# Reordering the start of a fused attention and GLU kernel: wo loaded early, fewer warm-ups, two clamps moved, a split wait

## The chip, the cores and the metric

The kernel runs on one core of one Trainium2 chip. The metric is the device time of one execution in microseconds (us): the median of the runs, less is better. Five engines work side by side, each through its own list of instructions in order: PE (TensorE, matmuls; its weight loads are shown as PEld), DVE (VectorE), ACT (ScalarE), POOL (GpSimd) and SP (SyncE, which here only issues DMA transfers). They wait for each other through semaphores.

## The reference

One sequence of 2048 tokens of width 448, all in bf16: a block of linear attention, then a GLU block, each behind a layer norm and with a residual.

```python
def _A_ref(x, wqkv, wo):                       # 16 heads of 28
    q, k, v = ...                              # x @ wqkv
    phi = lambda t: jnp.where(t > 0, t + 1, jnp.exp(t)) + 1e-6
    pq, pk = phi(q), phi(k)
    kv = jnp.einsum("bhsd,bhse->bhde", pk, v)
    z = jnp.einsum("bhsd->bhd", pk)
    num = jnp.einsum("bhqd,bhde->bhqe", pq, kv)
    den = jnp.einsum("bhqd,bhd->bhq", pq, z)[..., None] + 1e-6
    return (num / den).transpose(...) @ wo
def _B_ref(x, w_gate, w_up, w_down):
    return (_gelu(x @ w_gate) * (x @ w_up)) @ w_down
h = x + _A_ref(_layernorm(x), A_wqkv, A_wo)
h2 = h + _B_ref(_layernorm(h), w_gate, w_up, w_down)
```

## The kernel before, in words

The tokens are cut into 16 tiles of 128. Every piece of work is a task with a name, and the table ORDERS at the top lists, for each engine in turn (PE, ACT, DVE, POOL, SP), the names in the order in which that engine issues them. Nothing else decides the order. What a task waits for follows from the buffers that it reads and writes: `_Graph.add` collects these, and `emit` puts a wait ahead of the task for each semaphore that it has not yet seen far enough. A task with `mw` places its waits inside itself: each buffer has the number of the matmul that needs it.

The names, in order of time (t is a tile):

- **Warm-up.** warm1 (16 small matmuls) and warm0 (WARM matmuls of 128 columns, L454) use ones only and feed nothing.
- **Loads.** dx0 to dx12 bring x on the sync queue, dwk and dwv the key and value weights on ACT's queue; dwq with dwq_t and dwq_u the query weights, pqones a row of ones for the divisor; dwo, dwo_t, dwo_u and dwo_s the four pieces of wo (336, 56, 56 and 336 KB), dwg and dwu the gate and up weights, dwd the down weights.
- **First norm.** bnst and bnag (DVE) give mean and variance, ln and rstd (ACT) the inverse deviation, negm (POOL) the negated mean, norm the normed tile xn (DVE for tiles 0 to 3, POOL for the rest), dup (ACT) a copy of its last columns. Tiles 0 to 3 are transposed on PE (tr, L495) and copied out by ACT (ev, L523); from tile 4 on a DMA transposes them (xT, L526).
- **Keys and values.** k and v (8 and 6 matmuls of 64 rows, in pairs on the two halves of the PE rows, L430) fill two PSUM banks per tile. ek (ACT) takes the exponential of the keys, cl (L566) clamps it, ph (DVE, L568) makes phi(k) in the tile pk; evv (ACT, L570) copies the values. acc (halves a and b) adds phi(k) times v into banks 6 and 7. The a and b halves write the same banks from the other row half, so a task that follows one of the other kind on the same banks waits until PE has finished that one. Below this is called a turn of the row halves. The same holds between k and v of a tile, qa and qb, woa and wob, nda and ndb.
- **Queries.** qa and qb give four groups of heads for 512 tokens. For the first three of eight such pairs eq (ACT), cq (POOL) and pq (DVE, L627) make phi(q); for the others eq and rq (ACT, L616, L617), then cq and pq (DVE, L618, L619). kz1 and kz2 (DVE) take the finished sums out of banks 6 and 7.
- **Attention output and second norm.** nd multiplies phi(q) with the sums, rd and om (DVE) divide; for tiles 0 and 1 PE transposes the result (tro), ACT copies it (evo), wo multiplies; hr (DVE, L660) adds the residual, hbnst and hbnag and hln and hrstd give the norm, normh the normed tile hn, and wrap (L695) copies its first 64 columns behind its last. trh (7 transposes, L702) and evh (ACT or DVE) bring tiles 0 and 1 into hnT. The other tiles go in pairs, with DMA transposes oT and hT, and with POOL for vpe, pow, hnegm and normh.
- **GLU.** gu computes gate and up of one chunk of columns into a pair of banks, of which there are two; ge (ACT, L830) takes the Gelu of the gate, hm (DVE, L832) the product; the next but one gu needs the pair back. tbl2 loads the Gelu table once, behind the exponentials up to eq14. down multiplies with the down weights, out (DVE) adds the residual, dout stores.

Of the kernel before, what the change touches and what calls it, by code (L numbers as in the profile page):

```python
# [7 lines left out]
ALU = mybir.AluOpType  # L8
# [53 lines left out]
)  # L62


class _Buf:
    __slots__ = ("name", "writer", "readers")

    def __init__(self, name):
        self.name = name
        self.writer = None  # L70
        self.readers = []


# [157 lines left out]
def bass_sequential_preLN__linear_attn_block__glu_gated_geglu__prompt_kernel(  # L231
    nc, A_x, A_wqkv, A_wo, B_x, B_w_gate, B_w_up, B_w_down, out, cfg=None
):
    cfg = dict(cfg or {})
# [7 lines left out]
    HN_R = 4  # L242
    HR = 8
    O_R = 4
    QCH = 512
    NQC = S // QCH
    N_PE_TR = 4
    STAT_GROUPS = [[0], [1], [2], [3]] + [[t, t + 1] for t in range(4, T, 2)]
    EV_DVE = cfg.get("ev_dve", ())
    N_DVE_NORM = cfg.get("n_dve_norm", 4)  # L250
    N_PE_A2 = 2
    B1_CHUNKS = [2, 2, 4, 4, 4]
    WARM = 38
    WARM2 = 8
# [658 lines left out]
```

## Time and profile before

| what | value |
|---|---|
| median of 3 runs | 196.42 us |
| the runs | 196.16, 196.42, 196.70 us |
| the profiled execution | 196.70 us, of which the span 194.9 us |
| PE busy | 190.3 us (98%) |
| DVE, ACT, POOL busy | 116.3, 78.2, 42.0 us |
| granted TensorE clock over the span | 0.999 |
| DMA traffic | 17.53 MB, mean 90 GB/s |

All times of the trace count from the start of the span. A row of the timeline gives the start, the length, the engine, the line in the source, the operation, the tile that it writes and those that it reads, and in brackets how long its engine stood idle before it and who ended that. The ends of matmuls are modelled, so a PE that is shown busy can hold short waits; they show as idle time of PEld. Instructions of one line in a row are merged into one row, with their number (x6).

### The profile page before, as it was taken

The numbers are of one execution on the slowest core, as the hardware profiler recorded it, in microseconds if no ns is written. First come the engines' busy times: TensorE is split into PE (matmuls) and PEld (weight loads), VectorE is DVE, ScalarE is ACT, GpSimd is POOL, SyncE is SP. The second block draws the span as 40 slices with busy tenths as digits, with TensorE's granted clock in tenths as the row PEclk, the third lists the DMA queues.
The fourth block names the chain that finished last, engine by engine and source line by source line (L and its number), as shares of the span: only waits on it lengthen the run. The fifth ranks groups of instructions, "written<-read, shape, count | busy, mean of one in ns | idle before, by whom it ended". The sixth has DMA issues, their size and how long they took to land.

```text
span 194.9 us, 5336 instructions
## 1 busy us (share of the span) xinstructions
PE 190.3 (98%) x2192; PEld 137.9 (71%) x2192; DVE 116.3 (60%) x301; ACT 78.2 (40%) x205; POOL 42.0 (22%) x90
## 2 busy tenths in 40 slices
PE   7999999999999999999999999999999999999994
PEld 7556658754588977976675577877778779899554
DVE  2989735368998946843967745756735443431512
ACT  3689866669784212220442441233232442411100
POOL 3099974300050310500500500500500000000000
PEclk9999999999999999999999999999999999999999
DMA  6944558999836052152062250172040000010111
GB/s 191 377 116 97 81 110 185 247 248 205 260 103 110 15 101 50 50 105 62 10 129 46 46 106 2 30 117 51 5 94 28 23 0 0 3 47 3 47 47 47
DMA packets 37256, 17.53 MB, mean 90 GB/s; under 512 B 28272, under 2 KB 36336, under 8 KB 37232
## 3 DMA queue, kind: packets, MB, share of 16 engines
q1 hardware_dynamic: 36352, 16.45, 36.8%
q10 hardware_dynamic: 880, 0.75, 1.2%
q8 instruction: 17, 0.28, 0.6%
q14 instruction: 7, 0.06, 0.1%
HBM read 8.72 MB, written 1.84 MB: 54 GB/s over the span
## 4 chain that ended last, share of the span: by engine, by line
PE 96%; issue 1%; ACT 1%; DVE 1%; POOL 0%; DVEq 0%; ACTq 0%; POOLq 0%
PE ps L430 87%; PE ps L780 6%; PE ps L454 2%; DVE x_sb L660 1%; PE ps L495 1%; ACT xn L617 1%; PE ps L681 0%; ACT xnT L523 0%; PE ps L672 0%; DVE x_sb L756 0%; POOL ones_bf L395 0%; POOL eps_t L398 0%; ACT pqT L616 0%; DVEq L196 0%; ACTq L196 0%
## 5 line engine op out<-in xcount | busy, mean ns | idle before, releaser
L430 PE MATMUL ps<-hnT,wgu_sb 64*128 64x512 bf16 (+1 forms) x980 | 90.4, 333 | 0.0
L430 PEld LDWEIGHTS ps<-hnT,wgu_sb 64*128 64x128 bf16 x980 | 64.5, 94 | 18.6 <-DVE hh L832 1.7
L830 ACT ACTIVATE gl<-ps 128x256 bf16<-128x256 f32 x112 | 36.9, 381 | 89.3 <-PE ps L430 88.2
L832 DVE TENSOR_TENSOR hh<-ps,gl 128x256 bf16<-128x256 f32 x112 | 42.5, 415 | 35.7 <-ACT gl L830 31.5
L430 PE MATMUL ps<-wd_sb,hh 64*128 64x448 bf16 x336 | 34.4, 349 | 0.0
L430 PEld LDWEIGHTS ps<-wd_sb,hh 64*128 64x128 bf16 x336 | 25.6, 94 | 6.2 <-DVE x_sb L756 0.2
L430 PE MATMUL ps<-wkv_sb,xnT 64*128 64x448 bf16 x192 | 22.4, 350 | 0.4 <-ACT xnT L523 0.4
L462 DVE BATCH_NORM_STATS2 st<-x_sb 128x6 f32<-128x448 bf16 x32 | 18.7, 611 | 2.6 <-DMA x_sb<-in_A_x_dram 2.6
L756 DVE TENSOR_TENSOR x_sb<-ps,x_sb 128x448 bf16<-128x448 f32 (+1 forms) x17 | 9.9, 591 | 16.6 <-PE ps L430 9.8
L474 POOL TENSOR_SCALAR ln<-mv 128x2 f32<-128x2 f32 x7 | 1.6, 223 | 75.0 <-DVE mv L463 74.9
L568 DVE SCALAR_TENSOR_TENSOR pk<-ps,tm 128x448 bf16<-128x448 f32 x16 | 9.8, 620 | 9.6 <-POOL tm L566 7.1
L430 PE MATMUL ps<-xnT,wq_sb 64*128 64x512 bf16 x112 | 14.9, 377 | 0.2 <-ACT xn L617 0.2
L430 PEld LDWEIGHTS ps<-wkv_sb,xnT 64*128 64x128 bf16 x192 | 10.1, 94 | 6.3 <-issue 0.8
L430 PE MATMUL ps<-wo_sb,oT 64*128 64x448 bf16 x98 | 12.1, 350 | 0.1
L660 DVE TENSOR_TENSOR x_sb<-ps,x_sb 128x448 bf16<-128x448 f32 x16 | 9.4, 618 | 4.6 <-PE ps L430 4.4
L780 PE MATMUL ps<-wd_sb,hh 128*128 128x448 bf16 (+1 forms) x70 | 10.8, 315 | 0.0
L566 POOL TENSOR_SCALAR tm<-e 128x448 bf16<-128x448 bf16 x16 | 8.9, 559 | 6.4 <-ACT e L565 5.5
L487 POOL TENSOR_SCALAR hn<-x_sb,nm,rs 128x448 bf16<-128x448 bf16 x14 | 10.0, 720 | 0.8 <-POOL rs L476 0.2
L565 ACT ACTIVATE e<-ps 128x448 bf16<-128x448 f32 x16 | 8.5, 541 | 3.5 <-PE ps L430 2.2
L780 PEld LDWEIGHTS ps<-wd_sb,hh 128*128 128x128 bf16 x70 | 6.7, 98 | 4.3 <-issue 0.4
L655 DVE TENSOR_TENSOR o_sb<-ps,rd 128x448 bf16<-128x448 f32 x16 | 9.4, 612 | 0.1
L570 ACT ACTIVATE v<-ps 128x448 bf16<-128x448 f32 x16 | 8.4, 542 | 2.1 <-PE ps L430 2.1
(69 smaller groups left out, 140.4 us busy)
## 6 DMA issues: line engine op xcount, KB each, us to landing
out_dram<-x_sb SPq DMA_DIRECT2D x15, 112.0 KB, 1.7
wgu_sb<-in_B_w_gate_dram SPq DMA_DIRECT2D x7, 224.0 KB, 6.1
wgu_sb<-in_B_w_up_dram SPq DMA_DIRECT2D x7, 224.0 KB, 6.4
wd_sb<-in_B_w_down_dram SPq DMA_DIRECT2D x1, 1568.0 KB, 8.3
x_sb<-in_A_x_dram SPq DMA_DIRECT2D x2, 448.0 KB, 5.3
wkv_sb<-in_A_wqkv_dram ACTq DMA_DIRECT2D x2, 336.0 KB, 3.7
x_sb<-in_A_x_dram SPq DMA_DIRECT2D x3, 224.0 KB, 4.2
wo_sb<-in_A_wo_dram SPq DMA_DIRECT2D x2, 336.0 KB, 4.4
```

The lines of the kernel that those rows point to most:

```text
L430: ins = e.matmul(o_, l_, r_, start=s_, stop=p_, **kw)
L462: op("dve", lambda e: e.bn_stats(st[:, t, :], src_ap), [b_src], [b_st[t]], "%sbnst%d" % ("" if mv is mv1 else "h", t), 0.53, key, after=after)
L487: return lambda e: e.tensor_scalar(dst, src[:, t, :], nm[:, t:t + 1], rs[:, t:t + 1], ALU.add, ALU.mult)
L565: act_exp(lambda e: e.activation(e1[:, ie, :], oK, AF.Exp), bank(bk), [b_e1[ie]], "ek%d" % t, _c_act(D), kk)
L566: op("pool", lambda e: e.tensor_scalar(tm1[:, ie, :], e1[:, ie, :], 1.0 + EPS, 0.0, ALU.min, ALU.max), [b_e1[ie]], [b_tm1[ie]], "cl%d" % t ...
L568: op("dve", lambda e: e.scalar_tensor_tensor(pk[:, i, :, 0:GW], psK3, EPS, tm1[:, ie, :].rearrange("p (g e) -> p g e", g=NG), ALU.max, ALU ...
L655: op("dve", lambda e: e.tensor_tensor(o_sb[:, so, oc:oc + D].rearrange("p (a e) -> p a e", e=28), nd3[:, :, 0:28], rd[:, i, :].unsqueeze(2 ...
L660: op("dve", lambda e: e.tensor_tensor(h_sb[:, u, :], ps[:, b, 0:D], x_sb[:, u, :], ALU.add), bank(b) + [b_x[u]], [b_h[u]], "hr%d" % u, 0.5 ...
L756: op("dve", lambda e: e.tensor_tensor(x_sb[:, t, c0:c1], ps[:, bk, c0:c1], h_sb[:, t, c0:c1], ALU.add), bank(bk) + [b_h[t]], [bo], "out%d% ...
L780: ins = e.matmul(ps[:, bk, c0:c1], hh[:, j, hsl(t)], wd_sb[:, j, c0:c1], start=(j == 0), stop=(j == NJ - 1))
L830: G.add("act", lambda e, gi=gi, cs_=cs_, psG=psG: e.activation(gl[:, gi, cs_], psG[:, cs_], AF.Gelu_apprx_tanh), r=bank(BK_G[i]), w=[b_glh ...
L832: op("dve", lambda e, dst=dst, srcU=srcU, srcL=srcL: e.tensor_tensor(dst, srcU, srcL, ALU.mult), bank(BK_U[i]) + [b_glh], [b_ar[j_][t % HR ...
```

## The change

Four edits of the source and a new table:

- dwo, dwo_t, dwo_u and dwo_s move from behind the last xT to the list of first loads, behind dwq_u; pqones and xT4 now follow them, and dwg0 follows xT15 directly. The data and its destination stay as they are.
- WARM goes from 38 to 33.
- cl14 and cl15 run on DVE; the operation is the same.
- trh waits in two places: for normh ahead of the first transpose, for wrap ahead of the seventh, the only one that reads the copied columns.
- ORDERS is new on every engine. On DVE, pkones moves ahead of the first bnst; on PE, acc3a, acc4a, acc8b, acc9b, acc10a, acc13a, acc14a and qb31 change places, among others; on ACT, ek15 comes before evv15 and eq14 behind evh0. The diff ends with one line of PE's list; the places that the prediction speaks of are shown there.

```diff
-    WARM = 38
+    WARM = 33
+    CL_DVE = cfg.get("cl_dve", (14, 15))
...
         dma(wq_sb[64:128, 3, 0:D], A_wqkv[384:448, 0:D], [b_wq[2]], "dwq_u", 64 * D * 2, first=True)
+        dma(wo_sb[:, 0:3, :], A_wo[0:384, :].rearrange("(g p) n -> p g n", p=128), [b_wo[0]], "dwo", 384 * D * 2, first=True)
+        dma(wo_sb[0:64, 3, :], A_wo[384:448, :], [b_wo[1]], "dwo_t", 64 * D * 2, first=True)
+        dma(wo_sb[64:128, 3, :], A_wo[0:64, :], [b_wo[2]], "dwo_u", 64 * D * 2, first=True)
+        dma(wo_sb[:, 4:7, :], A_wo[64:448, :].rearrange("(g p) n -> p g n", p=128), [b_wo[3]], "dwo_s", 384 * D * 2, first=True)
...
         prev = xts[-1:]
-        prev = [dma(wo_sb[:, 0:3, :], A_wo[0:384, :].rearrange("(g p) n -> p g n", p=128), [b_wo[0]], "dwo", 384 * D * 2, after=prev, key=19.0)]
...
-            op("pool", lambda e: e.tensor_scalar(tm1[:, ie, :], e1[:, ie, :], 1.0 + EPS, 0.0, ALU.min, ALU.max),
-               [b_e1[ie]], [b_tm1[ie]], "cl%d" % t, 0.53, kk)
+            op("dve" if t in CL_DVE else "pool", lambda e: e.tensor_scalar(tm1[:, ie, :], e1[:, ie, :], 1.0 + EPS, 0.0, ALU.min, ALU.max),
+               [b_e1[ie]], [b_tm1[ie]], "cl%d" % t, _c_dve(D, 4.0) if t in CL_DVE else 0.53, kk)
...
-            def ftrh(e):
+            def ftrh(e, W):
                 ins = None
-                for k in (0, 1, 2, 4, 5, 6, 3):
+                for n, k in enumerate((0, 1, 2, 4, 5, 6, 3)):
+                    if n in (0, 6):
+                        W(n)
...
-            G.add("pe", ftrh, r=[b_hn[sh], b_hnd[sh], b_ident], w=bank(bh), name="trh%d" % t, dur=_c_mm(128, 7), key=ka)
+            G.add("pe", ftrh, r=[b_hn[sh], (b_hnd[sh], 6), b_ident], w=bank(bh), name="trh%d" % t, dur=_c_mm(128, 7), key=ka, mw=True, pdt=_c_mm(128))
...
-    " v5 k6 qa01 v6 qb01 k7 acc3a acc4a v7 acc4b acc5b k8 acc5a acc6a v8 k9 k10 v9 v10 qa10 acc6b acc7b qb10 acc7a"
+    " v5 acc3a k6 qa01 v6 qb01 acc4a k7 acc4b acc5b v7 k8 acc5a acc6a v8 k9 k10 v9 v10 qa10 acc6b acc7b qb10 acc7a"
```

More of the change, by code (lines that the diff above doesn't have):

```diff
@@ L15 @@
     "warm1 warm0 tr0 tr1 k0 v0 k1 tr2 tr3 v1 k2 acc0a k3 v2 v3 qa00 acc0b acc1b qb00 k4 acc1a acc2a v4 k5 acc2b acc3b"
[4 rows of a table removed]
[4 rows of a table added]
     " wo6b down0b nd8a gu11 nd8b gu10 gu13 gu12 down2a wo8a down2b wo8b gu15 nd10a gu14 nd10b gu17 gu16 gu19 gu18 gu21"
     " wo10a wo10b gu20 nd12a gu23 nd12b gu22 gu25 gu24 gu27 gu26 wo12a down4a wo12b gu29 nd14a gu28 nd14b gu31 down4b"
[40 rows of a table removed]
[31 rows of a table added]
+    "ones eps mhalf mones powwarm ident mask_a opad mask_b mask_c negm4 cl0 norm4 norm5 negm6 cl1 norm6 norm7 negm8"
[8 rows of a table added]
 )
@@ L531, in bass_sequential_preLN__linear_attn_block__glu_gated_geglu__prompt_kernel @@
         prev = xts[-1:]
-        prev = [dma(wo_sb[:, 0:3, :], A_wo[0:384, :].rearrange("(g p) n -> p g n", p=128), [b_wo[0]], "dwo", 384 * D * 2, after=prev, key=19.0)]
-        prev = [dma(wo_sb[0:64, 3, :], A_wo[384:448, :], [b_wo[1]], "dwo_t", 64 * D * 2, after=prev, key=19.0)]
-        prev = [dma(wo_sb[64:128, 3, :], A_wo[0:64, :], [b_wo[2]], "dwo_u", 64 * D * 2, after=prev, key=19.0)]
-        prev = [dma(wo_sb[:, 4:7, :], A_wo[64:448, :].rearrange("(g p) n -> p g n", p=128), [b_wo[3]], "dwo_s", 384 * D * 2, after=prev, key=19.0)]
         for k in range(7):
```

83 rows, old and new, of the table ORDERS are left out of this document.

## The prediction

> **What bounds the kernel now.** First the page: the span, and the engines' shares of the chain that ended last. Then the view by stretches (start:end, length, then busy time and instructions of PE, PEld, DVE, ACT and POOL, granted clock, DMA share, GB/s).
>
> ```profile
> span 194.9 us, 5336 instructions
> PE 96%; issue 1%; ACT 1%; DVE 1%; POOL 0%; DVEq 0%; ACTq 0%; POOLq 0%
> 0.00:12.00 12.00, 10.53 (x136) 7.68 (x138) 7.89 (x25) 6.99 (x20) 3.82 (x17) 1.00 0.80 261
> 12.00:30.00 18.00, 18.00 (x230) 10.93 (x226) 13.05 (x30) 14.83 (x46) 16.40 (x32) 1.00 0.54 90
> 30.00:55.00 25.00, 24.42 (x300) 14.99 (x297) 17.10 (x41) 18.28 (x29) 3.98 (x7) 1.00 0.94 237
> 55.00:180.00 125.00, 124.88 (x1455) 96.50 (x1451) 73.69 (x199) 37.44 (x112) 17.84 (x35) 1.00 0.24 49
> ```
>
> PE carries 96% of the chain. From 55 to 180 us it misses 0.12 us, so the many reordered names of the second half have nothing to win there. What can move lies before 55: 1.47 us without PE work up to 12 us, and 0.58 us between 30 and 55. Inside "busy" PE time lie some more short waits, which show as idle time of the weight loads (PEld). I take the change's places in order of time.
>
> **1. Five fewer warm-ups.** Rows of the timeline (start, length, engine, line): the warm-ups, norm0, the memset of pk, rstd1, norm1, tr0 with tr1, k0, tr2 with tr3, and for later use a DVE copy with the PE operation that waited for it.
>
> ```profile
> 1.93 4.24 PE L454 MATMUL ps<-ones_bf 128*128 128x128 bf16 x38
> 5.21 0.37 DVE L486 TENSOR_SCALAR xn<-x_sb,mv,rs 128x448 bf16<-128x448 bf16 x1
> 5.58 0.27 DVE L399 MEMSET pk<- 128x256 bf16 x1
> 5.66 0.20 ACT L469 ACTIVATE rs<-ln 128x1 f32<-128x1 f32 x1
> 5.97 0.40 DVE L486 TENSOR_SCALAR xn<-x_sb,mv,rs 128x448 bf16<-128x448 bf16 x1
> 6.10 0.96 PE L495 MATMUL ps<-ident,xn 64*128 64x64 bf16 x20
> 7.43 0.74 PE L430 MATMUL ps<-wkv_sb,xnT 64*128 64x448 bf16 x6 [0.36 <-ACT xnT L523]
> 9.76 0.75 PE L495 MATMUL ps<-ident,xn 64*128 64x64 bf16 x20
> 51.95 0.18 DVE L695 COPY hn<-hn 128x64 bf16<-128x64 bf16 x1
> 52.15 0.78 PEld L702 LDWEIGHTS ps<-ident,hn 128*128 128x128 bf16 x14 [0.37 <-DVE hn L695]
> ```
>
> norm0 is done at 5.21 + 0.37 = 5.58, but tr0 starts at 6.10, behind the warm-ups. Five of them take 5 x 4.24/38 = 0.56 us, so their end would allow 5.54. PE answers a finished DVE operation in 0.02 us (51.95 + 0.18 to 52.15). So tr0 starts at 5.60, 0.50 earlier, and now waits for norm0. Behind it on PE stand tr1 and k0, and k0 also waits for ev0, ScalarE's copy of tr0's result (the 0.36 us of idle time in its row): all of it moves with tr0, and k0 goes from 7.43 to 6.94, **+0.49**. tr1 gains less, as norm1 needs rstd1, done at 5.86: the memset moved out from ahead of norm1 (0.27 us, now in DVE's idle time before the first x tile) frees nothing. But tr1 at 6.39 still serves k1 in time, which stands behind k0 and v0.
>
> This holds for the profiled execution, where the tensor engine ran slowly until after tr1: 0.112 us per 128-column warm-up, and tr0 with tr1 took 0.96 us where tr2 with tr3, the same work, took 0.75. The clock column reads 1.00 there, so the rows decide. In an execution that reaches the fast rate during the warm-ups, these end earlier by themselves and the five are worth less, down to nothing. The three runs spread from 196.16 to 196.70, and the profiled one is the slowest. [...]
>
> **2. wo ahead of the first transpose.** The sync queue, before and after, from wq on (DMA rows; the transposes are xT4 to xT15):
>
> ```order
> L364 DMA wq_sb<-in_A_wqkv_dram 64x448 x2
> L364 DMA pqT<-ones_bf 1x64x128
> L526 DMA_TRANSPOSE xnT<-xn 128x4x128 x12
> L364 DMA wo_sb<-in_A_wo_dram 128x3x448
> L364 DMA wo_sb<-in_A_wo_dram 64x448 x2
> L364 DMA wo_sb<-in_A_wo_dram 128x3x448
> L364 DMA wgu_sb<-in_B_w_gate_dram 64x1792
> ```
> ```order
> L365 DMA wq_sb<-in_A_wqkv_dram 64x448 x2
> L365 DMA wo_sb<-in_A_wo_dram 128x3x448
> L365 DMA wo_sb<-in_A_wo_dram 64x448 x2
> L365 DMA wo_sb<-in_A_wo_dram 128x3x448
> L365 DMA pqT<-ones_bf 1x64x128
> L531 DMA_TRANSPOSE xnT<-xn 128x4x128 x12
> L365 DMA wgu_sb<-in_B_w_gate_dram 64x1792
> ```
>
> Four loads now stand ahead of xT4, and the gate and up weights directly behind xT15.
>
> ```profile
> 9.50:10.50 1.00, 1.00 (x28) 0.66 (x24) 0.53 (x2) 1.00 (x5) 0.56 (x1) 1.00 1.09 374
> 11.00:13.00 2.00, 2.00 (x26) 1.10 (x26) 2.00 (x8) 1.92 (x7) 2.00 (x5) 1.00 0.01 3
> 6.88 0.60 SPq L364 DMA_DIRECT2D pqT<-ones_bf  x1
> 11.65 10.30 SPq L526 DMA_TRANSPOSE xnT<-xn  x7
> 15.52 0.79 PE L430 MATMUL ps<-wkv_sb,xnT 64*128 64x448 bf16 x6
> L364 SPq DMA_DIRECT2D wo_sb<-in_A_wo_dram x4: 487/594/1370, 28.6 to 31.2; - x4
> DMA to landing us min/median/max: 2.4/2.5/4.1
> ```
>
> Issuing costs 4 x 0.6 = 2.4 us of the sync queue, from 6.88 to about 9.3, before xT4 can be issued (11.65, or 11.2 in step with k0). The data is 784 KB, 0.80 MB, at 374 GB/s 2.1 us. The engines are full until nearly 11 and empty from 11 to 13 (3 GB/s), so wo ends at about 12.9. xT4 lands 2.5 us after issue, at 13.7 to 14.2; the wanted k4 is at 15.52 - 0.49 = 15.03. Bounds: nothing, if the issue and the bulk overlap; 0.4 us, if all 2.5 us came behind 12.9. I take **0**, nearer to the former, as most of the 2.5 us is issue (1.2 us or more each: 10.30 for 7). Later, wgu comes 3.2 us sooner, but nobody waits for it: PE lists no wait for a DMA at all.
>
> **3. The chain of clamps into k6.** Everything that feeds k6 must move up too, and GpSimd has little room (16.40 of 18 us busy from 12 to 30). The clamps cq1 and cq0, DVE's pq1 and pq0, two negm, and k6's weights:
>
> ```profile
> 16.75 1.19 POOL L626 TENSOR_SCALAR tm<-e 112x512 bf16<-112x512 bf16 x2
> 17.39 1.29 DVE L627 SCALAR_TENSOR_TENSOR pqT<-ps,tm 112x512 bf16<-112x512 f32 x2
> 17.91 0.40 POOL L481 TENSOR_SCALAR nm<-mv 128x2 f32<-128x2 f32 x2
> 18.74 0.12 PEld L430 LDWEIGHTS ps<-wkv_sb,xnT 64*128 64x128 bf16 x4 [0.29 <-DVE pqT L627]
> ```
>
> k6 takes its banks from pq1 and pq0 (17.39 + 1.29 = 18.68) and starts at 18.74. GpSimd works through without a break from cl1 on, and the new order puts the same operations ahead of cq0 as the old one, and negm12 besides (0.40 / 2 = 0.20). If its chain starts 0.49 sooner, as cl0 and norm4 hang on k0 and v0, cq0 ends at 16.75 + 1.19 - 0.49 + 0.20 = 17.65 and pq0, half of 1.29 and a hand-over of 0.1 behind it, at 18.4. PE would reach k6 at 18.74 - 0.49 = 18.25, or at 18.37 with acc3a's four matmuls, which now stand ahead of it (half of the 0.23 us that eight such loads take in step 4). With the answer time k6 starts at about 18.5: **-0.13** (bounds 0, and -0.4 if GpSimd's chain gains nothing by k0).
>
> **4. The last two clamps, 36 to 41 us.** DVE at the end of the K tiles (L566, L568, L642 and L643 of before are clamp, pk, kz1 and kz2):
>
> ```order
> L568 SCALAR_TENSOR_TENSOR pk<-ps,tm 128x4x112 x5
> L642 TENSOR_TENSOR kvz<-ps,mask 113x16x28
> L643 TENSOR_TENSOR kvz<-ps,mask 113x16
> ```
> ```order
> L569 SCALAR_TENSOR_TENSOR pk<-ps,tm 128x4x112 x3
> L567 TENSOR_SCALAR tm<-e 128x448
> L569 SCALAR_TENSOR_TENSOR pk<-ps,tm 128x4x112
> L567 TENSOR_SCALAR tm<-e 128x448
> L569 SCALAR_TENSOR_TENSOR pk<-ps,tm 128x4x112
> L644 TENSOR_TENSOR kvz<-ps,mask 113x16
> L643 TENSOR_TENSOR kvz<-ps,mask 113x16x28
> ```
>
> The two clamps come onto DVE, each ahead of its pk, and on ScalarE ek15 changes places with evv15. Rows: evv14 with evv15, ek15, cl15, ph15, qa20's weights, the weights of acc12b, and the copy group of DVE (busy, mean ns).
>
> ```profile
> 37.08 0.98 ACT L570 ACTIVATE v<-ps 128x448 bf16<-128x448 f32 x2
> 37.93 0.56 ACT L565 ACTIVATE e<-ps 128x448 bf16<-128x448 f32 x1
> 38.58 0.56 POOL L566 TENSOR_SCALAR tm<-e 128x448 bf16<-128x448 bf16 x1 [0.75 <-ACT e L565]
> 39.27 0.62 DVE L568 SCALAR_TENSOR_TENSOR pk<-ps,tm 128x448 bf16<-128x448 f32 x1 [0.68 <-PE ps L430]
> 38.11 0.12 PEld L430 LDWEIGHTS ps<-xnT,wq_sb 64*128 64x128 bf16 x4 [0.25 <-ACT v L570]
> 37.59 0.23 PEld L430 LDWEIGHTS ps<-v,pk 64*128 64x128 bf16 x8 [0.22 <-PE ps L430]
> L749 DVE COPY hn<-hn 128x448 bf16<-128x448 bf16 x14 | 3.5, 273 | 1.0 <-POOL hn L487 0.9
> ```
>
> No row shows the clamp on DVE; the copy of the same size takes 0.27 us and norm0, above, 0.37. With 0.27 (its operands are constants, so it is nearer to the copy), the clamp saves 0.29 us and the hand-over of 0.13 between 39.14 and 39.27, and ek15's new place half of the 0.85 between 37.08 and 37.93: ph15 ends at 39.0 and not at 39.89. But PE did not wait so long for it. qa20 waits for evv15 (38.11), which now comes behind ek15 and so about 0.44 us **later**. Behind qa20 stand two acc halves less (13a and 14a are now ahead of it, 0.12 each as above), and no turn between acc15b and acc15a (0.22, paid earlier, beside that wait, between acc13b and acc13a): 0.24 + 0.22 - 0.44 gives **+0.02** (bounds -0.2 if the earlier turn is not hidden, and +0.3 if evv15 comes in time).
>
> **5. The late wait, 49 to 57 us.** PE from the last wo of tiles 2 and 3 to the first gate and up matmuls:
>
> ```order
> L430 MATMUL ps<-wo_sb,oT 128x448 x8
> L430 MATMUL ps<-xnT,wq_sb 128x512 x6
> L430 MATMUL ps<-wo_sb,oT 128x448 x6
> L702 MATMUL ps<-ident,hn 128x128 x14
> L430 MATMUL ps<-kvz,pqT 128x116 x16
> ```
> ```order
> L435 MATMUL ps<-wo_sb,oT 128x448 x14
> L705 MATMUL ps<-ident,hn 128x128 x14
> L435 MATMUL ps<-xnT,wq_sb 128x512 x6
> L435 MATMUL ps<-kvz,pqT 128x116 x16
> ```
>
> qb31 (six matmuls) moves behind the hn transposes and fills the wait ahead of nd4a. Rows: the weights of nd4a and of wo4b, eq14, the table load, the first Gelu, and the group of q matmuls.
>
> ```profile
> 53.47 0.21 PEld L430 LDWEIGHTS ps<-kvz,pqT 49*128 49x128 bf16 x7 [0.34 <-DVE x_sb L660]
> 62.84 0.12 PEld L430 LDWEIGHTS ps<-wo_sb,oT 64*128 64x128 bf16 x4 [0.50 <-PE ps L430]
> 51.69 1.02 ACT L616 ACTIVATE pqT<-ps 112x1024 bf16<-112x1024 f32 x1 [0.35 <-PE ps L430]
> 54.08 1.28 ACT L850 ACT_TABLE_LOAD   x1
> 55.87 0.66 ACT L830 ACTIVATE gl<-ps 128x256 bf16<-128x256 f32 x2 [0.50 <-PE ps L430]
> L430 PE MATMUL ps<-xnT,wq_sb 64*128 64x512 bf16 x112 | 14.9, 377 | 0.2 <-ACT xn L617 0.2
> ```
>
> The wait of 0.34 us goes. But wo2a and wo2b now adjoin and pay a turn as wo4a and wo4b do (0.50), so the hn transposes move up by 6 x 14.9/112 - 0.50 = 0.3 us, and gu1 by some 0.1. The seventh transpose alone now waits for its wrap copy, which DVE does behind normh0; it comes while the other six run, and trh0 and qb31 queue behind it for less than 0.2. What decides is ScalarE. evh0 ended at the table load's start, 54.08, and now ends at 53.78; eq14 (1.02) has moved in between, so the table load runs from 54.8 to 56.1 and not to 55.36, and the first Gelu starts 0.2 us later than 55.87 did. gu3 needs the bank that this Gelu and its product free; so the 0.1 is lost: **0** (bounds -0.25 and +0.35).
>
> **Sum.** 0.49 + 0 - 0.13 + 0.02 + 0 = 0.38 us on the profiled execution, 196.70 (its span 194.9 and 1.8 around it): 196.32. On a run like the lowest, 196.16, the first term is gone: 196.16 + 0.13 - 0.02 = 196.27. Both lie near 196.3, so I forecast **196.3**, against a median of 196.42. A measurement of this kernel can tell about 0.3%, 0.59 us, from no change: this is inside.
>
> **The rivals.**
> - More is won (195.6, chance 0.25): k6 finds its banks free, and of the waits in 4 and 5 the 0.22 and 0.34 us go without new ones: 196.70 - 0.49 - 0.22 - 0.34. For: DVE has idle time in 36 to 41. Against: the turns and the table load above.
> - The gain is eaten by xT4 or k6 (196.7, 0.12): 0.4 us more at either place, on 196.3.
> - The clock rises one step late (197.8, 0.13): with the warm-ups ending 0.5 us sooner, the slow rate lasts past k0. k0, v0 and k1 fill the time from 7.43 to 9.76, 2.33 us; at half rate that much more at most, less what their own waits hide, and nothing if the rate rises at k0: I take 1.5, on 196.3. [...] For: the rate was still slow in tr0, at 6.10, four us after the first warm0 matmul. Against: the gap ahead of k0 shrinks as well. [...]
>
> **How the numbers follow.** The forecast has 0.50. Faster by over 0.3%, under 195.83: 0.25. Slower, over 197.01: 0.13. Within: 0.50 + 0.12 = 0.62. The range, 195.4 to 197.0, takes in the first two rivals and the bounds of steps 2 to 5, and leaves out the late clock and a tail below, under 0.2.
>
> **What would show it.** tr0 at 5.6 waiting for DVE and k0 at 6.9; no PE wait at k4; k6 waiting for L628; ph15 0.9 us earlier but qa20 held by ScalarE's v copy; the table load ending 0.5 us later. Wrong, if k0 to k1 take twice their time, if xT4 lands after 15, or if PE loses more than 0.2 us anywhere after 57 us.

## The result, and the profile after

The changed kernel is slower: 197.02 us (median of 8 runs, 196.90 to 197.58) against 196.41 us (8 runs, 196.16 to 196.71). The ratio is 1.0035, with a 95% interval of 1.0025 to 1.0045, and so 0.6 us where the prediction had -0.1. The profiled execution is one of 197.04 us with a span of 195.3.

First the page of the changed kernel (its span), then the view by stretches, with the columns as before:

```profile
span 195.3 us, 5326 instructions
```
```profile
0.00:12.00 12.00, 9.72 (x137) 6.60 (x139) 8.32 (x26) 7.60 (x23) 4.82 (x20) 1.00 0.92 295
12.00:30.00 18.00, 17.28 (x222) 9.55 (x219) 12.04 (x28) 14.06 (x42) 15.53 (x29) 1.00 0.56 99
30.00:55.00 25.00, 24.52 (x304) 15.14 (x302) 17.91 (x44) 17.73 (x29) 2.87 (x5) 1.00 0.90 213
55.00:180.00 125.00, 124.76 (x1447) 87.35 (x1444) 74.28 (x198) 37.88 (x112) 18.56 (x35) 1.00 0.26 49
```

From 12 to 30 us PE was never without work before; now it misses 0.72 us. The stretch from 30 to 55 improves by 0.1, and the one from 55 to 180, in which the prediction saw nothing to win, loses 0.12. (The 0.8 us less PE work up to 12 us are mostly the warm-ups that are gone or ran faster.) The timeline shows the two places of the loss. The start, k4 and the sync queue:

```profile
1.93 2.95 PE L459 MATMUL ps<-ones_bf 128*128 128x128 bf16 x33
5.25 0.36 DVE L491 TENSOR_SCALAR xn<-x_sb,mv,rs 128x448 bf16<-128x448 bf16 x1
5.67 0.41 PE L500 MATMUL ps<-ident,xn 64*128 64x64 bf16 x10 [0.79 <-DVE xn L491]
6.46 0.41 PE L500 MATMUL ps<-ident,xn 64*128 64x64 bf16 x10 [0.38 <-DVE xn L491]
6.88 0.74 PE L435 MATMUL ps<-wkv_sb,xnT 64*128 64x448 bf16 x6
...
6.92 2.40 SPq L365 DMA_DIRECT2D wo_sb<-in_A_wo_dram  x4
9.36 0.59 SPq L365 DMA_DIRECT2D pqT<-ones_bf  x1
11.10 6.28 SPq L531 DMA_TRANSPOSE xnT<-xn  x4
...
15.86 0.74 PE L435 MATMUL ps<-wkv_sb,xnT 64*128 64x448 bf16 x6 [0.72 <-ACT v L571]
```

k0 starts at 6.88, 0.55 earlier than before. k4 starts at 15.86, 0.34 later. So the 0.55 is won and 0.89 is lost between the two, and the row of k4 shows the wait: 0.72 us. The row names ScalarE's value copy as the one that came last. The view of the transfers issued between 11.0 and 11.9 us speaks against that name (a row: form, count, then the time from issue to landing):

```profile
xnT<-xn SPq DMA_TRANSPOSE x1, 4.6
```

xT4, issued at 11.10, took 4.6 us and not the usual 2.5: it landed at 15.7, 0.15 us ahead of k4. The copy that k4's banks need is that of tile 2, done at 14.48; the last copy before k4 is that of tile 3, done at 15.73, on other banks. The first experiments test which of the two it was.

The second place is gu5, a gate and up chunk (rows of weights, DVE and POOL, first after, then before):

```profile
57.07 1.99 POOL L492 TENSOR_SCALAR hn<-x_sb,nm,rs 128x448 bf16<-128x448 bf16 x2
58.35 0.29 DVE L752 COPY hn<-hn 128x448 bf16<-128x448 bf16 x1
58.56 1.04 DVE L620 TENSOR_TENSOR pqT<-xn,pqT 112x1024 bf16<-112x1024 bf16 x1
59.52 0.26 DVE L752 COPY hn<-hn 128x448 bf16<-128x448 bf16 x1
59.71 0.74 DVE L835 TENSOR_TENSOR hh<-ps,gl 128x256 bf16<-128x256 f32 x2
60.51 1.42 PEld L435 LDWEIGHTS ps<-hnT,wgu_sb 64*128 64x128 bf16 x27 [0.40 <-DVE hh L835]
```
```profile
57.11 1.41 POOL L487 TENSOR_SCALAR hn<-x_sb,nm,rs 128x448 bf16<-128x448 bf16 x2
58.55 0.45 DVE L749 COPY hn<-hn 128x448 bf16<-128x448 bf16 x2
58.92 0.68 DVE L619 TENSOR_TENSOR pqT<-xn,pqT 112x1024 bf16<-112x1024 bf16 x1
59.52 0.75 DVE L832 TENSOR_TENSOR hh<-ps,gl 128x256 bf16<-128x256 f32 x2
```

The new table puts the product pq10 (1.04 us) and a second wrap copy directly ahead of the products hm3_1 and hm3_0. These start at 59.71 and not at 59.52, while PE reaches gu5 earlier; its weights wait 0.40 us, and 0.3 us of PE time is lost. Against the trace of before, PE stands at -0.21 us at gu1, at +0.17 at the wo matmuls behind gu5, at +0.23 at wo10b, and at +0.34 from down12 on, behind a wait at gu54 that is 0.10 longer (0.28, before 0.18).

### The profile page after: what moved, and what is told of

It is laid out like the page before. It is cut to its first block, busy times and chain, and to the rows that moved or that the text cites. A ratio compares the mean times of both kernels' runs of the same rounds, so it can differ in the third digit from the quotient of the medians.

```text
span 195.3 us, 5326 instructions
## 1 busy us (share of the span) xinstructions
PE 189.1 (97%) x2187; PEld 126.2 (65%) x2187; DVE 117.1 (60%) x303; ACT 77.9 (40%) x205; POOL 41.8 (21%) x88
## 4 chain that ended last, share of the span: by engine, by line
PE 85%; ACT 3%; DVE 2%; issue 1%; POOL 1%; DVEq 0%; ACTq 0%
PE ps L435 79%; PE ps L783 6%; DVE hh L835 1%; ACT L853 1%; ACT xn L618 1%; ACT pqT L617 0%; ACT hnT L710 0%; PE ps L705 0%; DVE pqT L620 0%; POOL xn L492 0%; PE ps L682 0%; PE ps L673 0%; POOL tm L567 0%; DVE pqT L619 0%; DVE hn L752 0%
## 5 line engine op out<-in xcount | busy, mean ns | idle before, releaser
L435 PE MATMUL ps<-hnT,wgu_sb 64*128 64x512 bf16 (+1 forms) x980 | 91.8, 333 | 0.1
L435 PEld LDWEIGHTS ps<-hnT,wgu_sb 64*128 64x128 bf16 x980 | 61.6, 94 | 23.0 <-DVE hh L835 5.1
L435 PE MATMUL ps<-wd_sb,hh 64*128 64x448 bf16 x336 | 35.2, 349 | 0.0
L435 PEld LDWEIGHTS ps<-wd_sb,hh 64*128 64x128 bf16 x336 | 20.9, 94 | 11.4 <-DVE x_sb L759 0.2
L435 PE MATMUL ps<-xnT,wq_sb 64*128 64x512 bf16 x112 | 14.5, 377 | 0.2 <-ACT xn L618 0.2
L435 PE MATMUL ps<-wo_sb,oT 64*128 64x448 bf16 x98 | 12.6, 350 | 0.2
L486 POOL TENSOR_SCALAR nm<-mv 128x2 f32<-128x2 f32 x13 | 2.9, 226 | 39.5 <-DVE mv L468 39.1
L492 POOL TENSOR_SCALAR hn<-x_sb,nm,rs 128x448 bf16<-128x448 bf16 x14 | 10.6, 762 | 0.8 <-POOL rs L481 0.2
L567 POOL TENSOR_SCALAR tm<-e 128x448 bf16<-128x448 bf16 x14 | 7.9, 562 | 4.8 <-ACT e L566 4.2
```

Of the source, the lines that this page charges most:

```text
L435: ins = e.matmul(o_, l_, r_, start=s_, stop=p_, **kw)
L492: return lambda e: e.tensor_scalar(dst, src[:, t, :], nm[:, t:t + 1], rs[:, t:t + 1], ALU.add, ALU.mult)
L567: op("dve" if t in CL_DVE else "pool", lambda e: e.tensor_scalar(tm1[:, ie, :], e1[:, ie, :], 1.0 + EPS, 0.0, ALU.min, ALU.max), [b_e1[ie] ...
```

## The experiments

Theory 1: wo's bulk holds xT4, and xT4 holds k4. Its rivals: ScalarE's copy (theory 2), the rise of the tensor engine's rate (theory 3), the order of VectorE at gu5 (theory 4). Theories 1 and 4 can both hold, as they speak of two places.

### wo put back, and wo moved alone

e1_wo_back is the changed kernel with this edit; e2_wo_early_only does the reverse to the kernel before.

```diff
-    "... dwq_u dwo dwo_t dwo_u dwo_s pqones xT4 ... xT15 dwg0 ..."
+    "... dwq_u pqones xT4 ... xT15 dwo dwo_t dwo_u dwo_s dwg0 ..."
```

> The changed kernel with wo's four loads back behind the last xT; all else as changed. Theory 1 (wo's bulk ahead of xT4 holds k4): xT4 lands near 13.7 us, k4 starts near 15.0 us without a wait, and of the 0.89 us lost at k4 some 0.5 stays to the end (part was regained by 36 us): 196.4 to 196.6 us against 197.02. Theory 2 (ScalarE's value copy evv3 holds k4, as the profile's row names it): k4 still at 15.8, 197.0 us. Step 3 of the prediction can be seen here too: k6 at about 18.5 waiting for pq0.

> The kernel before with wo's four loads moved ahead of xT4 and nothing else. Theory 1: xT4 lands about 1.5 us later than 14.0, at 15.5, k4 starts near 15.9 instead of 15.52 and the time goes up by 0.2 to 0.4 us, to 196.6 to 196.8. Theory 2: k4 at 15.5, 196.4 us.

Measured: e2 197.37 us (196.97 to 197.96), its kernel before 196.61; ratio 1.0044, interval 1.0030 to 1.0058. wo alone costs 0.8 us, twice the most that was expected, and the profile of e2 now names the transfer at k4:

```profile
16.25 0.74 PE L434 MATMUL ps<-wkv_sb,xnT 64*128 64x448 bf16 x6 [0.94 <-DMA xnT<-xn]
```

With wo put back, k4 starts without a wait at 14.99, where theory 1 had it:

```profile
14.99 0.80 PE L431 MATMUL ps<-wkv_sb,xnT 64*128 64x448 bf16 x6
```

So theory 2 is out: the name in the row of k4 was only that of the last event ahead of it. But e1 is not faster, it is the slowest of all: 198.32 us (197.16 to 199.81), ratio 1.0086 (1.0058 to 1.0113). The expectation of 196.4 to 196.6 failed. In the profiled execution (197.73 us) the time is lost elsewhere, at wo2a (rows of PE and of the sync queue, and the view of the transfers issued from 44.5 us on):

```profile
25.32 6.20 SPq L527 DMA_TRANSPOSE xnT<-xn  x4
31.58 2.38 SPq L365 DMA_DIRECT2D wo_sb<-in_A_wo_dram  x4
42.91 0.60 SPq L365 DMA_DIRECT2D wgu_sb<-in_B_w_up_dram  x1
44.78 2.51 SPq L732 DMA_TRANSPOSE oT<-o_sb  x2
...
50.26 0.35 PE L431 MATMUL ps<-wo_sb,oT 64*128 64x448 bf16 x1 [0.71 <-DVE mv L464]
50.79 1.72 PE L431 MATMUL ps<-wo_sb,oT 64*128 64x448 bf16 x13 [0.18 <-DMA oT<-o_sb]
```
```profile
oT<-o_sb SPq DMA_TRANSPOSE x2, 5.0
```

It is the same thing once more: transposing DMAs (oT2 and oT3) behind bulk loads (the gate and up weights) on one queue take 5.0 us in the middle, in place of 2.8 in the changed kernel. The last weights are issued at 42.91 and not at 40.91, since the new table brings GpSimd's norm12 late: xT12 goes out at 25.32 (23.46 before), xT15 at 30.3 (27.4 before). In the changed kernel nothing of this shows, because wo's 2.4 us of issue are gone from that place. Why the nine runs of e1 spread over 2.6 us stays open.

### The late norms

e6_wo_back_norms_early tests that: e1 with these orders on GpSimd (and the copies dup11 to dup15 to match) as in the kernel before.

```diff
-    "... cl4 norm13 cl5 norm10 negm14 norm11 cl6 opad2 cq3 cq2 cl7 norm12 norm14 cl8 norm15 ..."
+    "... cl4 norm10 norm11 cl5 norm13 norm12 cl6 negm14 cq3 cq2 cl7 norm14 opad2 norm15 cl8 ..."
```

> The changed kernel with wo back behind xT15 (the first experiment, 198.32 us) and, besides, GpSimd's norms and ScalarE's copies of tiles 11 to 15 in the order of the kernel before (norm12 ahead of the clamp of tile 6, not behind that of tile 7). Theory 1: xT15 is issued near 27.5 and not 30.3 us, wo and the gate and up weights 2.8 us sooner, the transposes oT2 and oT3 land by 49.4, the 0.9 us of waits at wo2a are gone: 196.2 to 196.9 us, and the runs spread less than from 197.16 to 199.81. If the loss of the first experiment came from another place: still above 197.7.

Measured: 196.72 us, inside what theory 1 expected; ratio 1.0025 (1.0004 to 1.0045). xT15 is issued at 27.4, oT2 and oT3 take 3.1 us, and the wait at wo2a is gone. Three of its eleven runs lie at 197.9 to 198.3, so the spread did not go as expected; what these are comes below.

### VectorE's order at gu5

```diff
-    "... hm0_0 wrap3 pq10 wrap2 hm3_1 hm3_0 pq12 pq14 ..."
+    "... hm0_0 wrap3 wrap2 hm3_1 hm3_0 pq10 pq12 pq14 ..."
```

> The changed kernel with one change of VectorE's order: pq10 moves from ahead of wrap2, hm3_1 and hm3_0 to behind them. Theory 4 (pq10 and the wrap copies ahead of hm3 hold gu5's bank and cost 0.3 us): gu5's wait of 0.295 us goes, wo4a starts 0.2 to 0.3 us sooner, 196.7 to 196.8 us against 197.02. Theory 1: k4 unchanged at 15.86, and if the time after 57 us is given back elsewhere, 197.0.

Measured: 196.95 us (196.60 to 197.72), ratio to the kernel before 1.0026, interval 1.0013 to 1.0038. This is above the 196.7 to 196.8 expected. In its profile the loss at gu5 falls from 0.295 to 0.027 us: theory 4 holds at that place. What the order is worth in time is not separated from the noise: the ratio of e4 and that of the changed kernel (1.0035) differ by 0.2 us with overlapping intervals, and so do those of e5 and e9 below, which differ in this order alone.

### The rate of the tensor engine

e3_warm33_only and e7_warm20_only are the kernel before with WARM = 33 and 20; e8_changed_warm38 is the changed kernel with WARM = 38.

> The kernel before with 33 instead of 38 warm-up matmuls and nothing else. If step 1 holds (k0 comes 0.49 us sooner where the clock rises late, nothing where it rises early): k0 near 6.9 us, the time 0.1 to 0.4 us lower, 196.0 to 196.3. Theory 3 (fewer warm-ups let the clock rise late in many runs, and that is the loss in the median): 196.7 to 197.5 us, with the runs spread wider than before's 196.16 to 196.71.

> The kernel before with 20 instead of 38 warm-up matmuls and nothing else. Theory 3 (the rival of the late clock: with a longer gap ahead of the transposes the tensor engine's rate rises later, in some runs only behind k0): a part of the runs, or all, at 197.5 to 198.5 us, and where the profile falls on one, tr0 to k1 at half rate (k0 near 1.5 us). If the three runs at 197.8 of the kernel with 33 warm-ups had another cause, the runs stay at 196.2 to 196.7.

> The changed kernel with 38 warm-ups again. Theory 1: k4 waits for xT4, whose landing does not depend on PE, so that the 0.5 us by which k0 moves are lost or won at k4 all the same: 197.0 to 197.1 us, with k0 at up to 7.4 and k4 still at 15.8. If the terms simply add up: 197.2 to 197.5 us.

Measured: e3 196.42 us, against 196.61, ratio 1.0014 (0.9994 to 1.0034); but of its eleven runs eight lie at 196.2 to 196.6 and three at 197.8 to 197.9. e7: 197.81 (197.64 to 198.59), ratio 1.0069 (1.0055 to 1.0083), all six runs high, and in its profiled execution k0 runs at the low rate (1.30 us for its first six matmuls, 0.74 at the high rate). e8: 197.38 (197.15 to 197.83), ratio 1.0041 (1.0029 to 1.0053); k0 is at 7.15 there and k4 at 16.14. The changed kernel has 1.0035 and, run again, 1.0033, so by these ratios 38 warm-ups cost it 0.1 to 0.2 us, between the two expectations; the intervals overlap, so this does not decide.

What a high run is shows in e5 (next part), whose profiled execution, 198.15 us, is one of them. k0, v0 and k1 in it, and in e9, 196.20 us, with the same 33 warm-ups:

```profile
7.06 1.30 PE L431 MATMUL ps<-wkv_sb,xnT 64*128 64x448 bf16 x6
8.13 0.60 PE L431 MATMUL ps<-wt_sb,xnT 64*128 64x448 bf16 x2
8.79 2.14 PE L431 MATMUL ps<-wkv_sb,xnT 64*128 64x448 bf16 x12
10.78 0.35 PE L431 MATMUL ps<-wt_sb,xnT 64*128 64x448 bf16 x2
```
```profile
6.98 0.74 PE L431 MATMUL ps<-wkv_sb,xnT 64*128 64x448 bf16 x6
7.54 0.37 PE L431 MATMUL ps<-wt_sb,xnT 64*128 64x448 bf16 x2
7.97 1.31 PE L431 MATMUL ps<-wkv_sb,xnT 64*128 64x448 bf16 x12
9.12 0.35 PE L431 MATMUL ps<-wt_sb,xnT 64*128 64x448 bf16 x2
```

k0, v0 and most of k1 run at a little over half the rate, and the same work ends 1.6 us later. With wo not ahead of xT4 and 33 warm-ups (e3, e5, e6, e9) 10 of 45 runs are as high, at 197.79 or above (e1, with its wide spread, is not counted; of the ten only that of e5 was profiled); of the 100 runs of the kernel before beside these experiments none is above 196.78. Theory 3 is thus real, and it was not the loss of the changed kernel: there every run lies at 196.9 or above, late rise or not. The moment of the rise differs between the profiled executions: the warm-up matmuls change from 0.107 to 0.056 us at 4.0 us in one (of the changed kernel), at 4.6 in another (e3), not at all in e5, where the rise comes some 10 us into the run. What sets that moment no row shows.

### Both repairs

e5_wo_in_gaps puts wo where the sync queue stood idle; e9_gaps_hm3 adds the order of e4; e10_gaps_hm3_warm38 has 38 warm-ups besides, e11_gaps_hm3_norms_warm38 the norms of e6 as well. e12_changed_again is the changed kernel beside them.

```diff
-    "... dwq_u dwo dwo_t dwo_u dwo_s pqones xT4 ... xT9 xT10 xT11 xT12 ..."
+    "... dwq_u pqones xT4 ... xT9 dwo xT10 dwo_s xT11 dwo_t dwo_u xT12 ..."
```

> The changed kernel with wo's four loads moved from ahead of xT4 into places where the sync queue stood idle: dwo behind xT9, dwo_s behind xT10, dwo_t and dwo_u behind xT11. Theory 1 (a transposing DMA lands only behind the bulk loads issued ahead of it on its queue; this held k4 in the changed kernel and wo2a in the kernel with wo put back): neither wait is left, xT4 lands near 13.7 and the second oT before 50 us, k4 starts near 15.0 and the time is 0.4 to 0.9 us under the changed kernel's 197.02, 196.1 to 196.6. Theory 2 (what was lost lies in the new order of the other engines): 197.0 or more.

> The changed kernel with wo's loads in the queue's idle places and pq10 behind hm3, the two repairs together. If the two losses (0.5 us at k4, 0.25 us at gu5) are all that the change lost, and add up: most runs at 196.1 to 196.4 us, gu5 without a wait, k4 without a wait, and about one run in four 1.4 to 1.6 us above, where the rate rises behind k0. If something else lost time as well: most runs at 196.5 or above.

> The same with 38 warm-ups. By theory 3 (33 warm-ups leave room for a late rise of the rate): no run more than 0.8 us above the lowest, the lowest runs not above those with 33, the median 196.2 to 196.5. If the high runs have another cause: again one in four at 197.5 or above.

> The same with 38 warm-ups and, besides, the norms of tiles 11 to 15 early as in the kernel before. If the late xT15 costs nothing once wo is out of its way: as without it, 196.2 to 196.5 us. If the transposes oT2 and oT3 still wait for the gate and up weights there: 0.2 to 0.4 us lower, 195.9 to 196.2.

> The changed kernel as it is, beside the three others on one chip. By theory 1 most runs lie at 196.9 to 197.2 us, 0.5 us or more above the kernel with both repairs, and since xT4 holds k4, a late rise of the rate costs less here than the 1.5 us there: the highest runs at 197.6 to 198.

| kernel | median (us) | runs | ratio to the kernel before, 95% |
|---|---|---|---|
| e5 wo in gaps | 196.59 | 9 of 12 at 196.3 to 196.8, 3 at 198.0 to 198.2 | 1.0017 (0.9996 to 1.0037) |
| e9 and hm3 first | 196.31 | 10 of 11 at 196.0 to 196.5, 1 at 197.84 | 0.9997 (0.9981 to 1.0013) |
| e10 and 38 warm-ups | 196.42 | 196.19 to 196.88 | 0.9999 (0.9990 to 1.0008) |
| e11 and early norms | 196.48 | 196.31 to 196.83 | 1.0003 (0.9994 to 1.0012) |
| e12 changed, again | 197.29 | 196.96 to 197.63 | 1.0033 (1.0020 to 1.0045) |

The last four are from one chip, with the kernel before at 196.44. The two repairs win 0.98 us over the changed kernel, all of its loss of 0.85 on this chip; whether they win more, the interval of e9 does not tell. e10 has no high run, as theory 3 expects. e11 is no better than e10: once wo is out of the way the late norms cost nothing that shows.

### What of the queue delays xT4

e13_pqones_first moves the 16 KB row of ones ahead of wo; e14_half_ahead, e15_small_ahead and e16_big_ahead leave only some of wo's pieces ahead of xT4. One execution each (197.00, 196.39, 197.83 and 196.80 us, with 196.72 for the kernel before), so the landings count here and not the times.

> The changed kernel with pqones, the 16 KB row of ones, ahead of wo's four loads and no longer between them and xT4. If the trickle of 24 GB/s is pqones: xT4 lands 0.6 us or more sooner, within 3.5 us of wq's landing. If it is the amount of data or wo's own pieces: xT4 still lands some 4.0 us behind wq, as in the changed kernel (11.71 to 15.72).

> The changed kernel with only dwo and dwo_t (392 KB) ahead of xT4, dwo_s behind xT9 and dwo_u behind xT11. By the amount of data (0.40 MB at the 290 GB/s seen while wo ran is 1.4 us): the data ends near 12.3, before xT4's issue does, and xT4 lands 2.4 us after its issue, at 13.7 to 14.2. If any load directly ahead of a transpose delays it: 14.5 or later.

> The changed kernel with only the two pieces of 64 rows, dwo_t and dwo_u (112 KB), ahead of xT4, the large ones behind xT9 and xT10. By the amount of data: xT4 at 13.7 to 14.2, not held. If the small pieces make the trickle: xT4 at 14.5 to 15.5.

> The changed kernel with only the two large pieces, dwo and dwo_s (672 KB), ahead of xT4, the small ones behind xT9 and xT10. By the amount of data (0.69 MB at 290 GB/s is 2.4 us, so 0.4 us less than all of wo): xT4 at 15.2 to 15.9. If the small pieces make the trickle: xT4 at 14.0 to 14.7.

| kernel | KB of wo ahead | wq landed | xT4 issued | xT4 landed | from issue |
|---|---|---|---|---|---|
| e9 | 0 | 12.11 | 11.21 | 13.81 | 2.6 |
| e15 | 112 | 12.56 | 12.61 | 15.18 | 2.6 |
| e14 | 392 | 11.84 | 11.17 | 15.07 | 3.9 |
| e16 | 672 | 11.90 | 11.38 | 15.52 | 4.1 |
| e13 | 784, not pqones | 12.00 | 11.37 | 15.69 | 4.3 |
| changed | 784 | 11.71 | 11.10 | 15.72 | 4.6 |
| changed, again | 784 | 12.09 | 11.32 | 16.30 | 5.0 |

Not the row of ones (e13). The small pieces alone delay nothing (e15, though xT4 was issued late there, in an execution with the late rate), and the delay grows with the bytes, but not in proportion: 672 KB (e16) land where the bytes put them, yet 392 KB (e14) already cost 1.3 us where the bytes allowed nothing, and xT4 there lands at 15.07 instead of 13.7 to 14.2. The view by stretches of the changed kernel shows a tail that the bytes don't:

```profile
11.00:13.50 2.50, 2.50 (x34) 1.36 (x30) 2.46 (x10) 2.29 (x9) 2.50 (x5) 1.00 1.12 316
13.50:15.00 1.50, 1.50 (x22) 0.65 (x18) 1.32 (x5) 1.27 (x5) 1.50 (x5) 1.00 0.93 68
15.00:15.50 0.50, 0.14 (x2) 0.00 (x0) 0.50 (x2) 0.46 (x2) 0.50 (x2) 1.00 0.99 213
```

The last two columns are the share of time in which the DMA engines had a packet, and GB/s. It looks as if xT4 were served only at 15.0, but the packets say otherwise. Here a transpose moved in 512 packets of 256 bytes, a row of wo in one of 896. Of the 576 small packets of xT4 and the row of ones, 540, fifteen sixteenths, went out by 13.84; those of 15.0 to 15.5 are mostly xT5's. In between wo's last rows go out one at a time, 0.04 us each, until 14.55, and the missing sixteenth of xT4 only behind them, from 14.56 on. I read this as one of the 16 DMA engines 1.3 us behind the others: from 13.3 on the 25 rows of wo that were left start one after the other, the last at 14.51. Two lines, of 13.90 to 14.55 and of 11.85 to 12.00, show this tail and what stands ahead of it, one 16 KB packet of the queue that the profile calls "instruction" (its time as a share of 16 engines' time in the window: 1.16 us):

```profile
DMA packets 42, 0.02 MB, mean 24 GB/s; under 512 B 25, under 2 KB 42, under 8 KB 42
q8 instruction: 1, 0.02, 48.3%
```

The kernel before has the same thing without any load ahead. xT15, issued at 27.37, took 3.7 us; nearly all its packets went out from 28.5 to 29.4, in which a 16 KB packet took 0.93 us, and the last sixteenth one at a time behind that (the landing, then 28.40 to 29.40, then 29.55 to 30.50):

```profile
xnT<-xn SPq DMA_TRANSPOSE x1, 3.7
DMA packets 501, 0.14 MB, mean 139 GB/s; under 512 B 500, under 2 KB 500, under 8 KB 500
q8 instruction: 1, 0.02, 5.8%
DMA packets 44, 0.01 MB, mean 9 GB/s; under 512 B 44, under 2 KB 44, under 8 KB 44
```

In e14 such a packet lasts from 12.20 to 13.42; the last row of wo, alone, starts at 13.40, and the last sixteenth of xT4 goes out behind it, until 14.3 (9 GB/s from 13.5 to 14.0, 13 from there to 14.5). This fits the 1.3 us that 392 KB cost. In e9 the packet (10.92, 1.33 us) is over before xT4's data starts at 12.5 (2 GB/s from 12.0 on, 201 from 12.5 on), and xT4 takes 2.6 us. No run moves the packet and the trace doesn't name the engine of a packet, so this reading rests on times that fit, and no experiment tests it.

### The fill, and a version that beats both

e17_fill is e9 with four more warm-up matmuls between tr0 and tr1; e18_fill_tail has, besides, gu50 to gu53 and what follows them in the order of before.

```diff
-    "warm1 warm0 tr0 tr1 k0 ..."
+    "warm1 warm0 tr0 warm2 tr1 k0 ..."
```

> The kernel with both repairs and 33 warm-ups (196.31 us, one run in eleven at 197.8) with four warm-up matmuls more, between tr0 and tr1, where PE waits 0.37 us for norm1; each takes 0.06 us at the high and 0.11 us at the low rate. If that gap lets the rate rise late: no run above 196.8, most at 196.0 to 196.4. If the gap does not matter: one to three runs of eleven at 197.5 or above again. If the four are in the way of tr1: most runs 0.1 us higher.

> The same, and the chunks gu50 to gu53 with their products and the outputs behind them in the order of the kernel before. The wait at gu54 goes from 0.28 to 0.18 us, the time is 0.1 us lower than without this, 195.9 to 196.3, and under the kernel before by 0.2 to 0.4 us. If the wait there has another cause: no difference.

Measured: e17 196.38 us, eleven runs at 196.12 to 196.78 and one at 197.32; ratio 0.9994 (0.9984 to 1.0005). e18 196.32 us, all eleven at 196.23 to 196.56, the kernel before beside them 196.62; ratio 0.9988, interval 0.9979 to 0.9997. None of the 23 runs with the fill lies at 197.8, of the 45 without it 10 did. That speaks for the gap ahead of tr1 as the cause, but four more warm-ups in any place were not tried, and one run at 197.32 is unexplained. e18 is the only version whose interval lies under the kernel before, by 0.1%, and so by some 0.5% under the changed one; at gu54 its loss is 0.19 us, as expected, but its 0.06 us under e17 is within the noise.

## Why the prediction was wrong, step by step

**Step 2, wo ahead of xT4, is the step that failed.** It took 0, between bounds of nothing and 0.4 us, with xT4 landing at 13.7 to 14.2. xT4 landed at 15.7 (16.3 when run again), and k4 lost 0.89 us in the profiled execution. The first error is the rate: wo was given 374 GB/s from the end of the bulk on, so an end at 12.9; the engines moved 316, and wo's rows went out side by side until 13.3. The second and larger is that the 16 engines were taken for one pipe: one of them ran 1.3 us behind, as far as the packets tell because of a 16 KB instruction packet (1.16 us), and the last sixteenth of xT4 went out only from 14.56 on, the rest by 13.84. The 4.1 in the prediction's own line of landings (2.4/2.5/4.1) is xT9 of the kernel before, which had such a packet beside it (19.40 to 20.89). Without that engine xT4 would have landed near 14.4 (an estimate: 13.84 and the 0.57 us from last packet to landing in e9; xT4 of the kernel before has 0.48), ahead of k4, and by this estimate the 0 would have held. The upper bound (all 2.5 us from issue to landing behind 12.9) was 15.4, and too low for the same reason. The prediction named "if xT4 lands after 15" as what would make it wrong, and its rival of 0.4 us at that place was the right mechanism with less than half of the price. The other half of step 2, "wgu comes 3.2 us sooner", failed as well: dwg0 was issued at 32.07, before 31.87, because xT15 goes out at 30.8 and not at 27.4. The step moved past a queue and forgot that the same table also moves what feeds that queue.

**Step 1** was right in the mechanism, but its number was met by luck: k0 came 0.55 us earlier, forecast 0.49, with tr0 at 5.67 waiting for norm0. In this execution the rate rose at 4.0 us, so the 33 warm-ups ended at 4.88 and 38 would have ended at about 5.16 (an estimate: five of 0.056 us more), both ahead of norm0's end at 5.61; the 0.55 is the early rise against the late one of the profile before, and not the five. That the step is worth less in other runs was right (0.2 us in the median of e3). In the changed kernel little of it arrives, since k4 waits for xT4, which does not depend on PE.

**Step 3** can be read only where wo is out of the way. In e9 pq1 and pq0 end at 18.45, forecast 18.4, and k6 starts at 18.50, forecast 18.5:

```profile
17.16 1.29 DVE L628 SCALAR_TENSOR_TENSOR pqT<-ps,tm 112x512 bf16<-112x512 f32 x2 [0.27 <-POOL tm L627]
```

In the changed kernel k6 starts at 19.10, behind the late k4, and finds its banks free.

**Step 4** was right in its rows: the clamp on VectorE takes 0.28 us (forecast 0.27), ph15 ends at 39.17 (39.0), and qa20 starts at 38.5, about when the value copy behind ek15 ends (38.53), though no row shows PE waiting for that copy. From k15 to qa11 the changed kernel wins 0.09 us, forecast 0.02. What no step counted is that the new PE order saves turns between 16 and 36 us: of the 0.34 us lost at k4 0.12 are left at k15 and none at wo0.

**Step 5** was right up to 57 us: the table load runs from 54.56 to 55.84 (forecast 54.8 to 56.1), gu1 starts 0.21 us sooner, and 0.09 of it goes at gu3. Behind it the prediction gave the second half up with one sentence, "nothing to win there". There was something to lose: pq10 ahead of hm3, 0.3 us, and 0.1 at gu54; a loss of over 0.2 us behind 57 us was one of its signs of being wrong. This is its second error: the reordered names were looked through for gains, where PE has none, and not for a new wait on VectorE, which PE meets at once when it has no slack.

The sum of the profiled execution against that of before: -0.55 at k0, +0.89 at k4, -0.36 up to wo0, -0.19 up to gu1, +0.38 at gu3 and gu5, +0.06 and +0.11 at wo10b and gu54; together +0.34. With the two losses taken out (e9) the time is 196.31, the 196.3 of the forecast, 0.13 us under the kernel before on that chip and not told from it by the interval. The rival of the late rate was right in effect and price (1.5 us, measured 1.4 to 1.6), in about a quarter of the runs of the repaired kernels. What sets the moment of the rise no run shows; of the 23 runs with four more matmuls between tr0 and tr1 none was that high. In the changed kernel, where no run is above 197.63, the wait for xT4 may cover most of it; no profiled execution of it shows the late rise.

## What to carry to other kernels

Before bulk loads are moved ahead on a queue, look for the next transfer on that queue for which somebody waits, and price it from the landing of the bulk's last piece, not from its bytes: wo was to end at 12.9 by its bytes, its last piece landed at 15.15, and xT4 behind it at 15.7. Put such loads into the idle places of the issuing queue instead. Where one engine carries 96% of the chain, a reordered stretch without idle time has nothing to win and all to lose: go through the other engines' new orders there for an operation that now stands ahead of one that frees a bank.

## What the runs showed of the hardware

In these traces a transposing DMA landed behind the loads issued ahead of it on its queue. xT4 of the changed kernel landed 0.2 us after the row of ones ahead of it (15.5), oT2 0.6 us after the last of the gate and up weights (48.0), and in the kernel before 0.5 us after them (48.4). The data itself did not wait for all of them: fifteen sixteenths of xT4 had gone out by 13.84, before wo's last row (14.51). What puts the landings in this order no row shows.

Some operations of GpSimd and VectorE took longer side by side. pq10, which reads xn and pqT, took 1.04 us beside normh2 and 0.63 (a third of 1.88) in e4, behind it:

```profile
57.69 2.00 POOL L492 TENSOR_SCALAR hn<-x_sb,nm,rs 128x448 bf16<-128x448 bf16 x2
60.72 1.88 DVE L620 TENSOR_TENSOR pqT<-xn,pqT 112x1024 bf16<-112x1024 bf16 x3
```

The two normh took 2.0 us in both, with two clamps of VectorE beside them (L619, 0.75 us), and 1.41 in the kernel before, where no clamp ran beside them. e4 moves pq10 alone and shows its 0.4 us; no run moves the clamps alone, and no row shows what the two engines share.
